# Attention and gated MoE on one core: TensorE's order in chunks 1 to 8 written by hand, a unit of attention every nine groups of products

## The chip, the cores and the metric

The kernel runs on one core of one Trainium2 chip. The metric is the device time of one execution in microseconds (us). Engines are named as in the profile: PE is TensorE (PEld its weight loads), DVE is VectorE, ACT is ScalarE, POOL is GpSimd, SP is the queue that issues the DMAs.

## The reference

q, k and v have the shape (8 batches, 8 heads, 576 tokens, 64). Attention is the sum of two parts, and its output x goes through a gated MoE layer.

```python
out_d = sm_attn(q_d, k_d, v_d)          # q, k, v averaged over 4 tokens: 144 each
out_up = np.repeat(out_d, 4, axis=2)
mask = np.abs(pos[:, None] - pos[None, :]) < 4
attn = softmax(where(mask, q @ k.T / 8, -1e9))
x = (out_up + attn @ v)                 # to (4608 tokens, 512)
gate = 1 / (1 + exp(-(x @ w_gate)))     # w_gate, w_val: 512 x 1536
return (gate * (x @ w_val)) @ w_out     # w_out: 1536 x 512
```

## The kernel before

**Attention** is done in 32 units, one for each pair of heads of a batch, four to a batch. A unit's work is cut into named steps: `prep2` (POOL sums q and k over four tokens), `s0` (PE: 48 small products, the local scores, then DVE adds the mask), `s1` and `sm` (softmax: DVE, POOL, ACT), `d0` (PE: 8 products, the scores `sd` of the averaged part, then DVE and ACT take their softmax), `dn`, `vd`, `v` (normalise; sum v; split v into two halves of 16 bits in `vblk`), `a0`, `a1` (PE transposes of the local softmax, into `at`), `at` (PE transposes of the averaged one, `adt`), `od` (PE: its product with v), and `x` (PE: the 30 products of the local softmax with `vblk`; DVE adds both parts into `xs`; ACT and POOL write two 16-bit halves of it to `xT`).

**MoE** is done in 9 chunks of 512 tokens. A chunk has 12 groups, and one group has three parts of 12 products with 512 columns: gate (`pg`), then value (`pv`), then output (`po`, for the group before). ACT takes the tanh of `pg` (L634), DVE multiplies it with `pv` (L642), ACT and DVE split the result (L650, L651), and `po` sums over the 12 groups. A chunk can begin once all units of its tokens have written `xT`: chunk 2 needs batch 2, chunk 3 batch 3, and so on to chunk 7, which needs batch 7.

**PSUM**: six banks belong to the MoE (`gate`, `val`, `o0` to `o3`). Attention's products of unit 4 and later, and the transposes that find a batch's largest v (`mxt`, in `max_all`), all take turns in two banks with the tag `att`. For the bound of a batch's v, `vmax` reads each unit's v on ACT, and after the fourth unit `max_all` makes a transpose, two DVE operations and a second product at once, and `pow2` and `inv_scaled` make the scales `pvb`, `svb`, `sxb` from it.

**Order.** Each step is put at a position, a number; the code emits the steps sorted by it. Chunk 0 lies below position `C1` = 56, with the conversion of the weights. From 56 on, each part of 12 products is one position: gate, value, output are 3, a chunk is 36, and chunk c begins at 56 + 36(c - 1). `base(u)` is a unit's position, and `offset(u, k)` that of its step k. The framework's scheduler decides at build time in which order every engine issues its instructions: the emitted order is a priority, and an instruction whose inputs or bank it holds to be late is overtaken by others. Loads go through SP, in three, one, one and five buffers for `qk`, `qkd`, `vd` and `v`.

`side_by_side` emits the small products of `s0` and `d0`, each tied behind the last, with one dummy product ahead of them (L404).

Of the kernel before, what the change touches and what calls it, by code (L numbers as in the profile page):

```python
# [10 lines left out]
F32 = mybir.dt.float32  # L11
I32 = mybir.dt.int32
AF = mybir.ActivationFunctionType
ALU = mybir.AluOpType
AX = mybir.AxisListType
# [1 line left out]

T = dict(ma=4.5, mas=0.45, mb=9.5, mbs=0.5, c1=56, gs=2.66, g0=16.84, r1=1.99, rs=1.6, ob=3.16, v0=15.13, v1=16.62, v2=17.5, vs=2.12, o0=18, os=1.2, pro=2.36, u4=13.82, u5=21, u6=27, u7=32, l4=1.3, l5=2.77, l6=9.47, l7=8.68, lv=15.08, vm=1.58, b8=6.75, s8=6.63, b12=26.05, s12=8.17, hold=32.07, al=0.76, am=1, z=3.68, sd=0, sn=0.79, v0m=0.61, xd=[2, 3, 7], ad=[0, 3, 7], aa=[0, 1, 2, 3, 6], td=[0, 3, 9, 10], vd=[0, 1, 2, 3, 6, 9, 10], a_prep2=-0.89, a_s0=0.01, a_s1=0.52, a_sm=1.82, a_d0=2.39, a_dn=5.17, a_a0=4.37, a_vd=4.6, a_a1=5.1, a_v=2.74, a_at=5.22, a_od=5.79, a_x=8.38, m_prep0=-3.14, m_prep2=-1.43, m_s0=0.69, m_s1=2.59, m_sm=3.12, m_d0=2.84, m_a0=10, m_dn=10.78, m_vd=11.67, m_a1=12, m_v=13.07, m_at=13.44, m_od=15.64, m_x=17, k0=30, k_prep2=0, k_s0=2, k_s1=2, k_sm=4, k_d0=3, k_dn=0, k_a0=3, k_vd=8, k_a1=2, k_v=5, k_at=0, k_od=0, k_x=0)  # L20
P = 128
B, H, S, D = 8, 8, 576, 64
NT = B * S
# [1 line left out]
NPAIR = H // 2  # L25
# [12 lines left out]
NCHUNK = NT // CH  # L38
NFC = DFF // P
# [11 lines left out]
VUP = 512.0  # L51
# [9 lines left out]
def attention_moe(ctx, tc, qk, qkd, v, vd, wg, wv, wo, mask, out):  # L61
    nc = tc.nc
# [55 lines left out]
    nc.vector.memset(ones, 1.0)  # L118


    def max_all(src, n):

        pt = ps_a.tile([P, 512], F32, tag="att", name=uniq("mxt"))
        nc.tensor.transpose(pt[:n, :P], src, ident)
        row = wk.tile([n, 1], F32, tag="mxr", name=uniq("mxr"))
        nc.vector.tensor_reduce(row, pt[:n, :P], axis=AX.X, op=ALU.max)
        dg = wk.tile([n, n], F32, tag="mxg", name=uniq("mxg"))  # L130
        nc.vector.tensor_scalar(out=dg, in0=ident[:n, :n], scalar1=row, scalar2=None, op0=ALU.mult)
        nc.tensor.matmul(pt[:, 256 : 256 + n], ones[:n, :].to_broadcast([n, P]), dg, start=True, stop=True)
        return pt[:, 256 : 256 + n]

    names = {}

    def uniq(k):
        names[k] = names.get(k, 0) + 1
        return f"{k}{names[k]}"

    def pow2(dst, src):

        got = max_all(src, src.shape[1])
        nc.vector.tensor_scalar(out=dst, in0=got, scalar1=TINY, scalar2=None, op0=ALU.max)
        nc.vector.tensor_scalar(
            out=dst.bitcast(I32), in0=dst.bitcast(I32), scalar1=EXPBITS, scalar2=None,
            op0=ALU.bitwise_and)

    def inv_scaled(dst, src, c):
        nc.vector.reciprocal(dst, src)  # L150
        nc.vector.tensor_scalar(out=dst, in0=dst, scalar1=c, scalar2=None, op0=ALU.mult)
# [145 lines left out]
    def vmax(u):  # L297
        b, hp = divmod(u, NPAIR)
        if hp == 0:
            vm[b] = wk.tile([P, NPAIR], F32, tag="vm", name=f"vm{b}")  # L300

        junk = wk.tile([P, NBLK * D], F16, tag="junk", name=f"junk_{u}", bufs=1)
        nc.scalar.activation(junk, vraw[u].rearrange("p a b -> p (a b)"), AF.Abs, accum_out=vm[b][:, hp : hp + 1])
        if hp == NPAIR - 1:
            m1 = wk.tile([P, 1], F32, tag="vm1", name=f"vm1_{b}")
            nc.vector.tensor_reduce(m1, vm[b], axis=AX.X, op=ALU.max)
            pow2(pvb[:, b : b + 1], m1)
            inv_scaled(svb[:, b : b + 1], pvb[:, b : b + 1], 2.0 * VUP)
            nc.vector.tensor_scalar(out=sxb[:, b : b + 1], in0=svb[:, b : b + 1], scalar1=4096.0 / VUP, scalar2=None, op0=ALU.mult)

    def batch_scales(b):
        nc.vector.tensor_scalar(
            out=tsc[:, b, :], in0=pw[:, 1::2], scalar1=pvb[:, b : b + 1], scalar2=2.0 ** -14,
            op0=ALU.mult, op1=ALU.mult)

    def out_scale(b):
        nc.vector.tensor_scalar(
            out=osc[:, b : b + 1], in0=qmax, scalar1=pw[:, 0:1], scalar2=pvb[:, b : b + 1], op0=ALU.mult, op1=ALU.mult)
# [82 lines left out]

    def side_by_side(other, mms):

        last = nc.tensor.matmul(other[:, 511:512], idle[:, :P], idle[:, :1], start=True, stop=True)  # L404
        for o, w, x in mms:
            with tc.issue_after(last.ins):
                last = nc.tensor.matmul(o, w, x, start=True, stop=True)  # L407

    owner = {}
    done = set()  # L410

# [213 lines left out]
    def moe_gate(c, fc):  # L625
        assert ("g", fc) in done
        assert all(u in done for u in range(min(NU, -(-(c + 1) * CH // S) * NPAIR))), (c, fc)
        x = xT[c]
        pt = ps_o.tile([P, CH], F32, tag="gate", name=f"pg_{c}_{fc}")
        for k in range(4):  # L630
            product(pt, [wg16[:, fc, a, k, :] for a in range(2)], [x[:, k, e, :] for e in range(2)], k == 0, k == 3)
        t = wk.tile([P, CH], F32, tag="tanh", name=f"tanh_{c}_{fc}")
        for b, o, n in segs_of_chunk(c):
            nc.scalar.activation(t[:, o : o + n], pt[:, o : o + n], AF.Tanh, scale=tsc[:, b, fc : fc + 1])  # L634
        return t
# [50 lines left out]
    def add(pos, f):  # L686
        steps.setdefault(pos, []).append(f)
# [6 lines left out]

    ALONE = {k[2:]: p for k, p in T.items() if k[:2] == "a_"}
    AMONG = {k[2:]: p for k, p in T.items() if k[:2] == "m_"}
    C1 = T["c1"]
    GSTEP = T["gs"]
    gt = {}
# [19 lines left out]
    def base(u):  # L719
        if u < NPAIR:  # L720
            return 1 + u * T["pro"]
        if u < 2 * NPAIR:
            return T[f"u{u}"]
        if u < 3 * NPAIR:
            return C1 - T["b8"] + (u - 2 * NPAIR) * T["s8"]
        return C1 + T["b12"] + (u - 3 * NPAIR) * T["s12"]

    def offset(u, k):
        if u < NPAIR:
            return ALONE[k] * T["al"]  # L730
        return AMONG[k] * (T["am"] if u < 2 * NPAIR else 1)

    for u in range(NU):
        b, hp = divmod(u, NPAIR)
        p0 = base(u)
        for k in ALONE if b == 0 else AMONG:
            add(p0 + offset(u, k), units[u][k])
            if b == 0 and T["k_" + k] and k in ("s0", "s1", "d0", "a0", "a1", "at", "od", "x"):
                add(p0 + offset(u, k), lambda n=T["k_" + k]: awake(n))
        if b == 0:  # L740
            if u == 0:
                add(-10, first_loads)
            add(2 + T["v0m"] * hp, lambda u=u: vmax(u))
            continue
        if b == 1:
            pl = p0 + offset(u, "prep0") - T[f"l{u}"]
            add(max(pl, base(u - 2) + offset(u - 2, "s1") + 0.1) if u > NPAIR + 1 else pl, lambda u=u: load_qk(u))
            add(T["lv"] + 0.2 * hp, lambda u=u: vload(u))
            after = base(u - 1) + 0.1 if u > NPAIR else 0
            add(max(pl + 0.5, after + offset(u - 1, "prep2") if after else 0), lambda u=u: load_qkd(u))  # L750
            add(max(pl + 0.5, after + offset(u - 1, "vd") if after else 0), lambda u=u: load_vd(u))
            add(T["lv"] + T["vm"] * (hp + 1), lambda u=u: vmax(u))
            continue
        add(base(u - 2) - 1 if b > 2 else max(base(u - 2) - 1, T["hold"]), lambda u=u: load_qk(u))
        add(base(u - 1) - 1 if u > 2 * NPAIR else T["hold"], lambda u=u: load_qkd(u))
        add(base(u - 1) + offset(u - 1, "vd"), lambda u=u: load_vd(u))
        pb = base(b * NPAIR)
        add(pb - 5 + hp, lambda u=u: vload(u))
        add(pb + hp, lambda u=u: vmax(u))

    worder.sort(key=lambda w: wpos(*w))
    add(RPOS, ratios)
# [3 lines left out]
    for n, (why, k, i) in enumerate(worder):  # L766
        add(wpos(why, k, i), lambda n=n: wstep(n))
    for b in range(1, B):
        add(max(base(b * NPAIR) + 5, C1 - 3), lambda b=b: (batch_scales(b), out_scale(b)))


    for fc in range(NFC):
# [6 lines left out]
    def run_steps(end):  # L779
        for p in sorted(p for p in steps if p < end):  # L780
            for f in steps.pop(p):
                f()
# [1 line left out]
    run_steps(C1)  # L784
    pos = C1
    prev = None
    for c in range(1, NCHUNK):
        for fc in range(NFC):
            t = moe_gate(c, fc)
            run_steps(pos + 1)  # L790
            moe_val(c, fc, t)
            run_steps(pos + 2)
            if prev is not None:
                moe_out(*prev)
            run_steps(pos + 3)
            pos += 3
            prev = (c, fc)
    moe_out(*prev)
    assert not steps


# [74 lines left out]
```

## Time and profile before

| | |
|---|---|
| median of 3 runs | 1142.66 us (1139.7 to 1144.16) |
| profiled execution, its own time | 1139.69 us |
| its span, first to last instruction | 1137.9 us |
| mean granted TensorE clock | 0.961 |
| busy: PE, DVE, ACT, POOL | 93%, 48%, 42%, 29% |

The profile is of one execution. A product's duration in it is longer than the distance to the next product, because products follow each other in a pipeline; the chain of waits gives the distance.

### The profile page before, as it was taken

To read this page: it belongs to the slowest core of one execution; us is meant where nothing else is said; L and a number is where in the kernel's file an instruction comes from. 1 tells how busy PE (TensorE), PEld (TensorE's weight loads), DVE (VectorE), ACT (ScalarE), POOL (GpSimd) and SP (SyncE) were. 2 spreads that over 40 slices of the span, in tenths; PEclk is the share of its full clock that TensorE was granted. 3 is DMA by queue.
4 is the path that set the end of the run, shared out by engine and by line. 5 is a ranking of instruction groups with operands and counts; after the bars stand their busy time and mean duration, and the time that the engine had idled before them with its cause. 6 is when DMAs were issued, how large, how long until landed. Compare 5 with 4: busy or idle time off the path is not lost.

```text
span 1137.9 us, 18103 instructions
## 1 busy us (share of the span) xinstructions
PE 1052.9 (93%) x7311; PEld 549.6 (48%) x7311; DVE 542.2 (48%) x954; ACT 482.1 (42%) x1176; POOL 335.5 (29%) x348
## 2 busy tenths in 40 slices
PE   6877788999996999899998999799989999999998
PEld 4753344545553555455444555455545554444443
DVE  5779999754436433543344433544354332122121
ACT  5734667533444443543444443534353443112112
POOL 6425546322235232332233233422343210000000
PEclk8659899999997999999999999999999999999999
DMA  9987675322114111321132211312120000000000
GB/s 348 391 298 242 236 247 180 138 103 68 57 60 153 52 53 55 114 75 61 64 105 70 69 54 64 127 48 69 57 90 19 1 1 38 1 1 38 1 1 37
DMA packets 32083, 110.48 MB, mean 97 GB/s; under 512 B 3584, under 2 KB 3840, under 8 KB 32000
## 3 DMA queue, kind: packets, MB, share of 16 engines
q1 hardware_dynamic: 32000, 109.33, 27.5%
q8 instruction: 57, 0.93, 0.3%
q14 instruction: 26, 0.21, 0.1%
HBM read 99.88 MB, written 9.44 MB: 96 GB/s over the span
## 4 chain that ended last, share of the span: by engine, by line
PE 80%; DVE 9%; ACT 4%; DMA 2%; POOL 2%; issue 2%; SPq 0%; DVEq 0%; ACTq 0%; POOLq 0%
PE po L400 23%; PE pg L400 23%; PE pv L400 22%; PE x L400 3%; PE od L400 2%; PE at L554 2%; PE s L407 2%; PE sd L407 1%; DVE wrv L209 1%; DVE wrv L210 1%; PE adt L565 1%; DMA v<-in_v_dram 1%; DVE vdblk L391 1%; DVE hmx L154 1%; ACT vblk L158 1%
## 5 line engine op out<-in xcount | busy, mean ns | idle before, releaser
L400 PE MATMUL pg<-xT,wg 128*128 128x512 f16 x1296 | 317.0, 387 | 21.7 <-ACT tanh L634 7.6
L400 PE MATMUL pv<-xT,wv 128*128 128x512 f16 x1296 | 310.9, 382 | 6.3 <-ACT wv L216 3.4
L400 PE MATMUL po<-g,wo 128*128 128x512 f16 x1188 | 278.7, 379 | 0.0
L400 PEld LDWEIGHTS <-wg 128*128 128x128 f16 x1296 | 124.7, 99 | 170.5 <-issue 23.5
L400 PEld LDWEIGHTS <-wv 128*128 128x128 f16 x1296 | 124.1, 98 | 154.4 <-issue 9.5
L400 PEld LDWEIGHTS <-wo 128*128 128x128 f16 x1296 | 123.9, 98 | 153.6 <-ACT wo L158 7.3
L642 DVE SCALAR_TENSOR_TENSOR tanh<-tanh,pv 128x512 f32<-128x512 f32 x108 | 73.7, 683 | 204.2 <-PE pv L400 192.7
L634 ACT ACTIVATE tanh<-pg,tsc 128x512 f32<-128x512 f32 (+7 forms) x192 | 86.6, 496 | 177.4 <-PE pg L400 177.2
L650 ACT ACTIVATE g<-tanh,gs 128x512 f16<-128x512 f32 x99 | 71.4, 721 | 151.9 <-DVE tanh L642 151.5
L651 DVE SCALAR_TENSOR_TENSOR g<-tanh,gs,g 128x512 f16<-128x512 f32 x99 | 81.8, 826 | 63.5 <-ACT g L650 63.0
L485 POOL TENSOR_TENSOR t<-t,mx 128x768 f32<-128x768 f32 x32 | 47.9, 1496 | 106.8 <-DVE mx L484 106.7
L597 DVE TENSOR_TENSOR xs<-x,od 128x464 f32<-128x464 f32 (+1 forms) x56 | 24.8, 455 | 95.1 <-PE x L400 94.8
L608 POOL TENSOR_TENSOR xT<-xs,xT 128x384 f16<-128x384 f32 (+7 forms) x54 | 45.5, 848 | 83.0 <-ACT xT L606 82.8
L496 POOL TENSOR_TENSOR t<-t,sm 128x768 f32<-128x768 f32 x28 | 46.3, 1654 | 72.8 <-DVE sm L494 65.3
L389 POOL TENSOR_TENSOR qkd<-qkd 128x576 f32<-128x576 f32 x29 | 36.2, 1248 | 80.9 <-DMA qkd<-in_qkd_dram 80.9
L158 ACT ACTIVATE vblk<-v,svb 64x640 f16<-64x640 f32 x48 | 39.6, 826 | 29.9 <-PE x L400 24.5
L391 POOL TENSOR_TENSOR vdblk<-vd 64x192 f32<-64x192 f32 x50 | 30.0, 600 | 72.1 <-PE od L400 66.7
L159 DVE SCALAR_TENSOR_TENSOR vblk<-v,svb,vblk 64x640 f16<-64x640 f32 x48 | 46.0, 959 | 11.0 <-ACT vblk L158 10.0
L474 DVE SCALAR_TENSOR_TENSOR t<-s,mk 128x384 f32<-128x384 f32 x64 | 32.8, 551 | 33.8 <-PE s L407 33.6
L539 POOL TENSOR_TENSOR ad<-e,sme 72x288 f32<-72x288 f32 x52 | 35.0, 693 | 45.8 <-PE adt L565 42.2
L522 ACT ACTIVATE e<-sd,mxd 72x144 f32<-72x144 f32 x128 | 47.0, 371 | 1.3
L491 DVE TENSOR_REDUCE sm<-t 128x12 f32<-128x768 f32 x32 | 30.4, 950 | 32.5 <-ACT t L486 32.5
(296 smaller groups left out, 1109.8 us busy)
## 6 DMA issues: line engine op xcount, KB each, us to landing
qk<-in_qk_dram SPq DMA_DIRECT2D x30, 610.0 KB, 4.2
qkd<-in_qkd_dram SPq DMA_DIRECT2D x29, 576.0 KB, 3.8
vd<-in_vd_dram SPq DMA_DIRECT2D x29, 384.0 KB, 3.0
v<-in_v_dram SPq DMA_DIRECT2D x32, 320.0 KB, 2.9
out_dram<-osb SPq DMA_DIRECT2D x16, 512.0 KB, 2.8
wo<-in_qk_dram SPq DMA_DIRECT2D x2, 610.0 KB, 9.8
wo<-in_qkd_dram SPq DMA_DIRECT2D x2, 576.0 KB, 9.2
out_dram<-osb SPq DMA_DIRECT2D x4, 256.0 KB, 2.3
```

What stands on the lines that cost most here:

```text
L158: nc.scalar.activation(hi, src, AF.Copy, scale=sc)
L159: nc.vector.scalar_tensor_tensor(out=lo, in0=src, scalar=sc, in1=hi, op0=ALU.mult, op1=ALU.subtract)
L391: eng.tensor_tensor(out=o, in0=x[ps, :, 0], in1=x[ps, :, 1], op=ALU.add)
L400: nc.tensor.matmul(o, w[a], x[c], start=first and i == 0, stop=last and i == len(pairs) - 1)
L485: nc.gpsimd.tensor_tensor(out=t, in0=t, in1=mx.unsqueeze(2).to_broadcast([P, 4 * NH, WIN]), op=ALU.subtract)
L496: eng.tensor_tensor(out=t, in0=t, in1=sm.unsqueeze(2).to_broadcast([P, 4 * NH, WIN]), op=ALU.mult)
L522: nc.scalar.activation(s["e"][:, qb, h, :], pt[:QM, qb * SD : (qb + 1) * SD], AF.Exp, bias=mx[:, qb : qb + 1], scale=QKSCALE / 16, accum_o ...
L608: eng.tensor_tensor(out=x[:, hp, 1, o : o + n], in0=src, in1=x[:, hp, 0, o : o + n], op=ALU.subtract)
L634: nc.scalar.activation(t[:, o : o + n], pt[:, o : o + n], AF.Tanh, scale=tsc[:, b, fc : fc + 1])
L642: nc.vector.scalar_tensor_tensor(out=t, in0=t, scalar=1.0, in1=pt, op0=ALU.add, op1=ALU.mult)
L650: nc.scalar.activation(g[:, 0], t, AF.Copy, scale=gs[:, fc : fc + 1])
L651: nc.vector.scalar_tensor_tensor(out=g[:, 1], in0=t, scalar=gs[:, fc : fc + 1], in1=g[:, 0], op0=ALU.mult, op1=ALU.subtract)
```

## The change

1. From chunk 1 on, the loop over chunks and groups stands in a region in which PE's instructions are issued in the order in which the code emits them. Other engines, and the place of PE instructions that are emitted before the region (chunk 0, units 4 to 7, the first steps of units 8 and 9), stay with the scheduler.
2. Units 8 to 31 begin every nine positions: `base(u)` = 44 + 9(u - 8). Before, units 8 to 11 were 6.63 apart from 49.25 on, and units 12 to 31 were 8.17 apart from 82.05 on.
3. Their steps take offsets of a new table, `STEADY`.
4. For batches 2 to 7 the bound of v is made in two steps: `vrows` (the transpose and two DVE operations) at 5.5 after the batch's first unit, and `vscale` (the second product, in a bank of its own, and the scales) at 6.65. Batch 1 keeps both at once; the scales of batches 2 to 7 for the MoE follow at 7 instead of 5.
5. In the region `side_by_side` has neither the dummy product nor the ties.

```diff
-... b8=6.75, s8=6.63, b12=26.05, s12=8.17, ...
+... b8=12, s8=9, ...
-    def max_all(src, n):
+    def max_rows(src, n):
         pt = ps_a.tile([P, 512], F32, tag="att", name=uniq("mxt"))
         nc.tensor.transpose(pt[:n, :P], src, ident)
...
+        return dg, pt
+    def spread(dg, n, pt=None):
+        if pt is None:
+            pt = ps_a.tile([P, 512], F32, tag="att", name=uniq("mxt"))
         nc.tensor.matmul(pt[:, 256 : 256 + n], ones[:n, :].to_broadcast([n, P]), dg, start=True, stop=True)
         return pt[:, 256 : 256 + n]
+        if hp == NPAIR - 1 and b < 2:
+            vrows(b)
+            vscale(b)
+    def vrows(b):
+        m1 = wk.tile([P, 1], F32, tag="vm1", name=f"vm1_{b}")
+        nc.vector.tensor_reduce(m1, vm[b], axis=AX.X, op=ALU.max)
+        vm[b] = max_rows(m1, 1)
+    def vscale(b):
+        pow2(pvb[:, b : b + 1], spread(vm[b][0], 1, vm[b][1] if b < 2 else None))
+        inv_scaled(svb[:, b : b + 1], pvb[:, b : b + 1], 2.0 * VUP)
...
-        last = nc.tensor.matmul(other[:, 511:512], idle[:, :P], idle[:, :1], start=True, stop=True)
+        last = None if ordered else nc.tensor.matmul(other[:, 511:512], idle[:, :P], idle[:, :1], start=True, stop=True)
         for o, w, x in mms:
+            if last is None:
+                nc.tensor.matmul(o, w, x, start=True, stop=True)
+                continue
...
+    STEADY = dict(prep0=0, prep2=-3.5, s0=0, s1=0.1, sm=1.1, d0=2, dn=6.1, vd=9.4, v=8.2,
+                  a0=13, a1=13, at=14.4, od=15.6, x=16.6)
-        if u < 3 * NPAIR:
-            return C1 - T["b8"] + (u - 2 * NPAIR) * T["s8"]
-        return C1 + T["b12"] + (u - 3 * NPAIR) * T["s12"]
+        return C1 - T["b8"] + (u - 2 * NPAIR) * T["s8"]
...
+        if hp == NPAIR - 1:
+            add(pb + 5.5, lambda b=b: vrows(b))
+            add(pb + 6.65, lambda b=b: vscale(b))
-        add(max(base(b * NPAIR) + 5, C1 - 3), lambda b=b: (batch_scales(b), out_scale(b)))
+        add(max(base(b * NPAIR) + (5 if b < 2 else 7), C1 - 3), lambda b=b: (batch_scales(b), out_scale(b)))
...
+    ordered.append(True)
+    with tc.manual_schedule(engines={mybir.EngineType.PE}):
         for c in range(1, NCHUNK):
```

## Rows read from the trace of the kernel before

**Rows 1.** The page: busy time (share of the span) and instructions of each engine

```profile
PE 1052.9 (93%) x7311; PEld 549.6 (48%) x7311; DVE 542.2 (48%) x954; ACT 482.1 (42%) x1176; POOL 335.5 (29%) x348
```

**Rows 2.** Windows by chunk: length; PE, PEld, DVE, ACT, POOL; clock; DMA, GB/s

```profile
231.90:346.80 114.90, 112.89 (x835) 57.87 (x834) 50.92 (x94) 49.03 (x128) 29.48 (x32) 1.00 0.24 80
346.80:482.90 136.10, 123.40 (x1012) 65.15 (x1012) 62.35 (x115) 59.98 (x157) 48.57 (x55) 0.95 0.23 77
482.90:601.10 118.20, 113.71 (x859) 59.61 (x859) 50.82 (x93) 52.40 (x135) 38.88 (x44) 0.99 0.23 77
601.10:721.80 120.70, 113.93 (x860) 58.81 (x860) 50.93 (x93) 52.26 (x135) 39.14 (x44) 0.99 0.22 73
721.80:841.40 119.60, 112.67 (x861) 58.54 (x861) 52.03 (x93) 51.72 (x133) 39.59 (x45) 1.00 0.22 73
841.40:951.90 110.50, 109.28 (x754) 56.34 (x753) 45.80 (x73) 44.88 (x114) 26.34 (x31) 1.00 0.05 17
951.90:1137.90 186.00, 181.46 (x840) 82.10 (x839) 37.04 (x52) 38.78 (x68) 0.63 (x1) 1.00 0.04 15
```

**Rows 3.** Chain of waits at the start of chunk 4: start, us, what

```profile
601.63 2.91 DMA v<-in_v_dram
...
605.39 0.74 ACT tanh L634 x2
...
606.17 4.44 PE pg L400 x12
```

**Rows 4.** Waits of PE from 231.9 on: total us, times, longest

```profile
PE pg L400 <- ACT tanh L634: 7.6, 6, 2.7
...
PE s L404 <- DVE xs L597: 6.3, 5, 3.8
PE mxt L132 <- DVE mxg L131: 3.0, 5, 0.6
```

**Rows 5.** Chain of waits through undisturbed units of chunk 2

```profile
420.41 0.65 PE x L400 x24
...
424.73 0.16 PE x L400 x6
...
429.45 0.86 PE s L407 x48
...
431.93 2.59 PE pg L400 x12
...
435.17 0.33 PE at L554 x3
...
440.70 0.65 PE sd L407 x8
...
447.60 0.38 PE adt L565 x6
...
452.73 0.73 PE od L400 x6
453.47 0.66 PE x L400 x24
```

**Rows 6.** Timeline: last reader of the score banks; a late reader of `at`

```profile
431.35 1.01 DVE L474 SCALAR_TENSOR_TENSOR t<-s,mk 128x384 f32<-128x384 f32 x2
...
443.42 0.36 ACT L522 ACTIVATE e<-sd,mxd 72x144 f32<-72x144 f32 x1
...
603.26 0.49 PE L554 MATMUL at<-ident,t 128*128 128x128 f32 x3
...
606.75 0.45 DVE L548 TENSOR_TENSOR at<-at,at 128x290 f16<-128x290 f32 x1
```

**Rows 7.** Chain of waits around the first gate of chunk 1

```profile
229.05 0.39 PE x L400 x4
...
233.77 0.86 PE s L407 x48
```

**Rows 8.** Timeline of SP near the last weight loads

```profile
194.25 0.42 SPq L286 DMA_DIRECT2D v<-in_v_dram  x1
```

More of the change, by code (lines that the diff above doesn't have):

```diff
@@ L16 @@
 PSUM = bass.MemoryType.PSUM
-T = dict(ma=4.5, mas=0.45, mb=9.5, mbs=0.5, c1=56, gs=2.66, g0=16.84, r1=1.99, rs=1.6, ob=3.16, v0=15.13, v1=16.62, v2=17.5, vs=2.12, o0=18, os=1.2, pro=2.36, u4=13.82, u5=21, u6=27, u7=32, l4=1.3, l5=2.77, l6=9.47, l7=8.68, lv=15.08, vm=1.58, b8=6.75, s8=6.63, b12=26.05, s12=8.17, hold=32.07, al=0.76, am=1, z=3.68, sd=0, sn=0.79, v0m=0.61, xd=[2, 3, 7], ad=[0, 3, 7], aa=[0, 1, 2, 3, 6], td=[0, 3, 9, 10], vd=[0, 1, 2, 3, 6, 9, 10], a_prep2=-0.89, a_s0=0.01, a_s1=0.52, a_sm=1.82, a_d0=2.39, a_dn=5.17, a_a0=4.37, a_vd=4.6, a_a1=5.1, a_v=2.74, a_at=5.22, a_od=5.79, a_x=8.38, m_prep0=-3.14, m_prep2=-1.43, m_s0=0.69, m_s1=2.59, m_sm=3.12, m_d0=2.84, m_a0=10, m_dn=10.78, m_vd=11.67, m_a1=12, m_v=13.07, m_at=13.44, m_od=15.64, m_x=17, k0=30, k_prep2=0, k_s0=2, k_s1=2, k_sm=4, k_d0=3, k_dn=0, k_a0=3, k_vd=8, k_a1=2, k_v=5, k_at=0, k_od=0, k_x=0)
+T = dict(ma=4.5, mas=0.45, mb=9.5, mbs=0.5, c1=56, gs=2.66, g0=16.84, r1=1.99, rs=1.6, ob=3.16, v0=15.13, v1=16.62, v2=17.5, vs=2.12, o0=18, os=1.2, pro=2.36, u4=13.82, u5=21, u6=27, u7=32, l4=1.3, l5=2.77, l6=9.47, l7=8.68, lv=15.08, vm=1.58, b8=12, s8=9, hold=32.07, al=0.76, am=1, z=3.68, sd=0, sn=0.79, v0m=0.61, xd=[2, 3, 7], ad=[0, 3, 7], aa=[0, 1, 2, 3, 6], td=[0, 3, 9, 10], vd=[0, 1, 2, 3, 6, 9, 10], a_prep2=-0.89, a_s0=0.01, a_s1=0.52, a_sm=1.82, a_d0=2.39, a_dn=5.17, a_a0=4.37, a_vd=4.6, a_a1=5.1, a_v=2.74, a_at=5.22, a_od=5.79, a_x=8.38, m_prep0=-3.14, m_prep2=-1.43, m_s0=0.69, m_s1=2.59, m_sm=3.12, m_d0=2.84, m_a0=10, m_dn=10.78, m_vd=11.67, m_a1=12, m_v=13.07, m_at=13.44, m_od=15.64, m_x=17, k0=30, k_prep2=0, k_s0=2, k_s1=2, k_sm=4, k_d0=3, k_dn=0, k_a0=3, k_vd=8, k_a1=2, k_v=5, k_at=0, k_od=0, k_x=0)
 P = 128
@@ L131, in max_all @@
         nc.vector.tensor_scalar(out=dg, in0=ident[:n, :n], scalar1=row, scalar2=None, op0=ALU.mult)
+        return dg, pt
+    def spread(dg, n, pt=None):
+        if pt is None:
+            pt = ps_a.tile([P, 512], F32, tag="att", name=uniq("mxt"))
         nc.tensor.matmul(pt[:, 256 : 256 + n], ones[:n, :].to_broadcast([n, P]), dg, start=True, stop=True)
         return pt[:, 256 : 256 + n]
+    def max_all(src, n):
+        dg, pt = max_rows(src, n)
+        return spread(dg, n, pt)
     names = {}
@@ L139, in uniq, with pow2 @@
         return f"{k}{names[k]}"
-    def pow2(dst, src):
-        got = max_all(src, src.shape[1])
+    def pow2(dst, got):
         nc.vector.tensor_scalar(out=dst, in0=got, scalar1=TINY, scalar2=None, op0=ALU.max)
@@ L303, in vmax @@
         nc.scalar.activation(junk, vraw[u].rearrange("p a b -> p (a b)"), AF.Abs, accum_out=vm[b][:, hp : hp + 1])
[L304 to L309, printed above, removed]
+        if hp == NPAIR - 1 and b < 2:
[8 more added lines that the diff above has]
+        inv_scaled(svb[:, b : b + 1], pvb[:, b : b + 1], 2.0 * VUP)
+        nc.vector.tensor_scalar(out=sxb[:, b : b + 1], in0=svb[:, b : b + 1], scalar1=4096.0 / VUP, scalar2=None, op0=ALU.mult)
     def batch_scales(b):
@@ L402, in side_by_side @@
     def side_by_side(other, mms):
-        last = nc.tensor.matmul(other[:, 511:512], idle[:, :P], idle[:, :1], start=True, stop=True)
+        last = None if ordered else nc.tensor.matmul(other[:, 511:512], idle[:, :P], idle[:, :1], start=True, stop=True)
         for o, w, x in mms:
+            if last is None:
+                nc.tensor.matmul(o, w, x, start=True, stop=True)
+                continue
             with tc.issue_after(last.ins):
                 last = nc.tensor.matmul(o, w, x, start=True, stop=True)
+    ordered = []
     owner = {}
@@ L696, in attention_moe @@
     AMONG = {k[2:]: p for k, p in T.items() if k[:2] == "m_"}
+    STEADY = dict(prep0=0, prep2=-3.5, s0=0, s1=0.1, sm=1.1, d0=2, dn=6.1, vd=9.4, v=8.2, a0=13, a1=13, at=14.4, od=15.6, x=16.6)
     C1 = T["c1"]
@@ L730, in offset @@
             return ALONE[k] * T["al"]
-        return AMONG[k] * (T["am"] if u < 2 * NPAIR else 1)
+        if u < 2 * NPAIR:
+            return AMONG[k] * T["am"]
+        return STEADY[k]
     for u in range(NU):
@@ L786, in attention_moe @@
     prev = None
[L787 to L798, printed above, removed]
+    ordered.append(True)
+    with tc.manual_schedule(engines={mybir.EngineType.PE}):
+        for c in range(1, NCHUNK):
+            for fc in range(NFC):
+                t = moe_gate(c, fc)
+                run_steps(pos + 1)
+                moe_val(c, fc, t)
+                run_steps(pos + 2)
+                if prev is not None:
+                    moe_out(*prev)
+                run_steps(pos + 3)
+                pos += 3
+                prev = (c, fc)
+        moe_out(*prev)
     assert not steps
```

## The prediction

> **What bounds the kernel now.** I read the page first: PE is busy 93% of the span and no other engine half of it [rows 1]. Then the windows from one chunk's first gate to the next [rows 2]. The six stretches of chunks 1 to 6 hold the same products, 36 x 12 = 432 each, and about four units each, yet they take 114.9, 136.1, 118.2, 120.7, 119.6 and 110.5 us. In the last one the chunks 7 and 8 run nearly without attention. So something other than products and attention fills up to 25 us of a chunk, and the second row also has a mean clock of 0.95. DVE, ACT and POOL are under 50% in all seven rows.
>
> The chain of waits says what. Inside a chunk it runs from PE instruction to PE instruction, 2.59 us for 12 products, with attention's pieces between them [rows 5]. At a chunk's start it leaves PE [rows 3]: the batch's last unit has only just been done, and the gate of chunk 4 waits for a tanh, which stood on ACT behind a read of v, whose load landed then. The 12 products after it take 4.44 us instead of 2.59: the window of that chunk has a mean clock of 0.99 [rows 2], so for part of them the clock stood on its lower level, 1.2 instead of 2.4 GHz, after PE had stood idle. The waits of PE name the same places [rows 4]: `pg` for tanh, `s` for `xs`, the two halves of `max_all` for each other.
>
> **What full work would take.** Chunks 1 to 8 have 96 groups of 36 products, 3456 in all. The last window holds 840 of them, so 2616 lie before it. At 2.59 / 12 = 0.2158 us that is 564.6 us. A unit costs, by its pieces, s 0.86, sd 0.65, two transposes of 0.33, adt 0.38, od 0.73, x 0.65 + 0.16: 4.09 us [rows 5]; 24 units, 98.2. Five bounds of v, two short pieces each, at the 0.33 of three transposes a piece: 3.3. Together 666.1 us, where the first six windows of rows 2 took 720.0. **53.9 us are lost** between 231.9 and 951.9. The last window is full already: 840 products in the 181.46 us that PE is busy there are 0.216 a product.
>
> The idle part of the loss is smaller than that: in the six windows PE is idle 720.0 - 685.9 = 34.1 us [rows 2]. The rest is time in which PE counts as busy and does half: the 12 products of 4.44 us lose 1.85 [rows 3]. The Trainium skill, in "Trainium Kernel Development and Optimization", section Performance Expectations, calls matmul busy time a bad metric because matmuls are pipelined. By the busy rows alone there would be 34 us to win and my sum below would end near 1118; the count of products gives 53.9, and the even last window bears the count out.
>
> **The change part by part.**
>
> *Spacing.* Units of 9 positions make four units exactly one chunk of 36. The fourth unit of batch 2 has x at 44 + 27 + 16.6 = 87.6, and chunk 2 begins at 92, and so with each later chunk. 4.4 positions are at least 4.4 x 2.59 = 11.4 us, for a tail of xs, cast and difference that took 2.5 us at chunk 1's start (x ends 229.44, the gate comes at 231.9) [rows 2, 7]. If the order holds, no gate waits for its unit. Loads: v's at -5 to -2 from a batch's start take buffers freed by a `v` step at -9.8 or earlier (five buffers, 9 apart). The wait of rows 3, in which ACT stands behind a load of v, goes too.
>
> *Fixed order.* Now every PE wait in the region is a wait of all that follows, so each place must have room. In steady state the two banks are used, in turn, by s at 0, sd at 2, the transposes of the unit before at 4, adt at 5.4, od at 6.6, x at 7.6, s again at 9. Between s and sd, and between sd and the transposes, lie two parts, 5.2 us; from transposes to adt, adt to od and od to x one part, 2.6 us. What the readers need: DVE finished with s 432.36 - 430.31 = 2.05 us after it; the last exp of sd ended 443.78, 2.43 after sd [rows 5, 6]. These fit twice over. The tightest is the bank of the transposes: the slowest reader that I found ended 607.20, 3.5 us after them (603.75) [rows 6], 0.9 over the room, but it stood behind the same late load of v. Inputs that come through long chains (softmax for `a0`, 13 positions, over 33 us after `s0`) have far more. So I put what is left at 0.2 us per unit, 24 x 0.2 = 5 us; bounds 0 and 1 us a unit, 0 to 24 us.
>
> *Dummy product and bound of v.* A unit loses two dummies of one column; at 0.86 / 48 = 0.018 us, the price of a small product of s [rows 5], all 48 are 0.9 us, which I leave out; no reason speaks for a loss. The two halves of `max_all` cost 0.6 us of waiting each time [rows 4]; with a gate part of 2.59 between `vrows` (5.5) and `vscale` (6.65) that is covered, and it is in the 53.9. An extra bank turn per batch falls between adt and od and needs one short DVE read. `svb` is needed by `v` at 8.2, 1.5 positions or 4 us after `vscale`, against a handful of small DVE operations (0.6 us for two with their waits, so some 2). If this cover were gone, ACT and DVE would be late with `vblk`, whose reader x comes 8.4 positions later: nothing for PE.
>
> *Earlier start of units 8 and 9.* This is the part with a cost. u8's `s0`, `d0` move from 49.9 and 52.1 to 44 and 46, u9's to 53 and 55: all below 56, and in the banks' turn ahead of unit 7's adt (45.44), od (47.64) and x (49). Now u8's s runs after u7's x, at 233.77, and those 2.5 us from u7's x to chunk 1's gate leave no slack [rows 2, 7]. In the new turn s takes 0.86, DVE frees its banks 2.05 after, sd takes 0.65, its exps 2.43: 6.0 us that u7's x can be later. PE has output parts of chunk 0 to fill it, but only those that it has now, so the delay shows at the gate. On the other side are waits hidden under fill, and 1.5 us of PE work done before. Then `a0` of unit 8, fixed two parts after chunk 1's first gate, waits in the region for the banks behind u9's s and sd, another 0 to 5 us. DVE has some 4 us more to do there (estimated as four passes like the 1.01 of rows 6); the steps between s and sd that hold the banks are in the 6.0 already, so I count at most 1. The loads of v for units 8 to 11 go out five positions earlier, ahead of more of the last weight loads on SP: an issue takes 0.42 us of SP [rows 8], so four delay those by 1.7 at most. Bounds together: a gain of 3 (s and sd of both units, 1.51 us each, in gaps that PE has now) to a loss of 6.0 + 5 + 1 + 1.7 = 13.7; between them I take a loss of 5, nearer the middle, since half of the bank delay can be covered.
>
> **Sum.** 231.9 + 666.1 + 186.0 = 1084.0; + 5 at the start of chunk 1; + 5 within the units: span 1094. The profiled execution takes 1.8 us over its span: 1096. The median of the three runs was 3.0 above the profiled execution; I forecast 1098 for the median.
>
> **Rivals.**
>
> *A. The hand-over costs more, or units leave more.* Loss of 13.7 at chunk 1 and 0.6 us per unit, 14.4: 1084.0 + 28 + 1.8 = 1114, to 1125 with the bounds. For it: the region cannot be overtaken, and unit 7 has no slack [rows 7]. Against it: the measured releases [rows 6].
>
> *B. Slower: the two banks can't turn in nine positions.* In the undisturbed stretch x of one unit lies 33.1 us before x of the next (the chain has it at 420.41 and 453.47), while nine positions and a unit make 9 x 2.59 + 4.09 = 27.4. If 33.1 is what the banks need, and not what the scheduler chose, a fixed order pays 5.7 us a unit, 137 us: 1084 + 5 + 137 = 1226 span, about 1229. It decides from a mean of (1137.9 - 1089) / 24 = 2.0 us a unit on. For it: the pieces there stand about two parts apart, as if each waited for a bank. Against it: the bank is free 2.0 to 2.5 us after the products [rows 5, 6], so the hardware wasn't what held them. The Trainium skill, "TensorE: Matmul & The Clock Gate", section Part 2, says that matmuls stay in program order and only weight loads are pulled ahead. The trace agrees: gates wait up to 2.7 us for tanh, and no other product fills that time [rows 4]. It holds in both kernels, and by it each wait in the fixed order costs in full.
>
> *C. No change.* The waits at chunk starts have moved into the units: the same 53.9, 2 us a unit, 1138 span, 1140 to 1143 median. For it: the tail of a batch's bound and of softmax could itself be late. Against it: DVE, ACT and POOL under 50% [rows 2].
>
> **Chances.** Forecast (1084 to 1106) 0.60; A (1106 to 1126) 0.22; C 0.08, half of it still 0.5% faster; B 0.07; better than 1084 0.03. I call 0.5% (5.7 us) what a measurement can tell. Faster 0.88, same 0.05, slower 0.07. The range that leaves out 2 in 10 reaches from 1084, where both charges are nothing, to 1122, into A; the likeliest case's own is 1084 to 1106.
>
> **What would show it.** Right: the windows by chunk become even, about 111 us for chunks 1 to 6 (93.2 of products, 16.4 of units, 0.7, and 0.8 of residue), with the last two unchanged; the lower clock gone after chunk 1's start; `pg` no longer waiting for tanh or xT; PE's idle time after 231.9 under 15 us. The start of chunk 1 lies near 235, and u8's s ahead of u7's adt. Wrong: `at`, `adt` or `sd` waiting over 1 us in every unit for a reader on DVE or ACT (B); the first gate of chunk 1 after 246 (A); chunks still at 118 us with small waits (C).

## The result, and the profile after

The changed kernel takes 1106.81 us (median of 4 runs, 1104.77 to 1107.43), the kernel before 1141.65 in the same comparison: ratio 0.9691, interval 0.9666 to 0.9715, so faster by 3.1%. The profiled execution took 1106.37 us, its span is 1104.6. The forecast was 1098, in a range of 1084 to 1122. The time lies inside the range, but just past the upper end of the likeliest case (1106), in the times that were given to rival A (1106 to 1126, chance 0.22).

The same line of the page as in [rows 1]: PE is busy 5.5 us less, the span is 33.3 shorter.

```profile
PE 1047.4 (95%) x7267; PEld 546.4 (49%) x7267; DVE 539.8 (49%) x954; ACT 476.6 (43%) x1176; POOL 348.4 (32%) x348
```

The windows from one chunk's first gate to the next, to be set beside [rows 2] (length; PE, PEld, DVE, ACT, POOL; clock; DMA, GB/s). Left out are chunks 3 to 5, which are like chunk 2. Output products of one chunk run in the window of the next, not at the same places as before, so only the rows of equal content (chunks 2 to 5) are read one by one.

```profile
230.00:360.60 130.60, 121.45 (x936) 64.48 (x934) 64.78 (x121) 55.92 (x149) 44.87 (x48) 0.93 0.25 83
360.60:471.60 111.00, 111.00 (x854) 57.86 (x853) 52.05 (x93) 51.78 (x134) 40.82 (x44) 1.00 0.24 80
...
804.40:911.50 107.10, 107.10 (x739) 55.39 (x738) 39.56 (x69) 42.60 (x110) 24.20 (x27) 1.00 0.06 20
911.50:1104.60 193.10, 189.19 (x877) 85.55 (x875) 38.19 (x54) 41.57 (x75) 0.00 (x0) 1.00 0.04 17
```

From chunk 2 to chunk 6 PE is busy for every microsecond, at a clock of 1.00, and chunks 2 to 5 last 110.9 to 111.0 us each, where before they took 118 to 136. Chunk 1 takes 130.6: there are 9.2 us of idle time and a mean clock of 0.93. The only other idle time is 3.9 us of the last window, which had 4.5 before. So what is still lost to waits is in chunk 1, at the hand-over from the part that the scheduler orders to the region of fixed order.

The waits of PE from 226 on (total us, times, longest), to be set beside [rows 4]; two more are of 0.4 and 0.2 us. None lies behind 263, so the three groups of rows 4 are gone and what is left belongs to the start of chunk 1:

```profile
PE at L571 <- ACT e L539: 4.1, 2, 2.4
PE sd L417 <- DVE t L491: 2.1, 1, 2.1
PE od L413 <- ACT e L539: 1.6, 1, 1.6
PE s L423 <- DVE pvb L150: 0.5, 1, 0.5
```

The chain of waits there (start, us, what), to be set beside [rows 7]:

```profile
223.57 0.86 PE s L423 x48
...
229.29 0.38 PE adt L582 x6
...
230.12 1.94 PE pg L413 x9
232.07 0.69 PE sd L423 x8
...
233.75 0.56 ACT e L539 x3
...
234.35 1.00 PE od L413 x6
235.35 2.83 PE x L413 x16
...
241.36 3.49 PE pv L413 x12
...
247.41 0.88 DVE vblk L165
248.29 0.93 DVE t L491 x2
...
254.44 0.73 ACT e L539 x4
...
255.22 0.90 PE at L571 x3
256.12 0.93 PE adt L582 x6
257.05 4.16 PE pg L413 x12
```

Unit 8's `s` (223.57) now runs ahead of unit 7's adt, and its `sd` ahead of unit 7's od and x. So od waits 1.64 us for the exp that reads `sd`, and x ends at 239.0, 9.6 later than before [rows 7]. The first gate doesn't wait for that: it starts at 230.0, since nine products of it go ahead of `sd`. Its last three wait for unit 7's `xT` and start at 239.67. The timeline of PE (start, us, line, output from inputs; in brackets the idle time before it and who ended it) has both:

```profile
235.30 3.72 PE L413 MATMUL x<-at,vblk 128*128 128x58 f32 x20
...
239.67 1.69 PE L413 MATMUL pg<-xT,wg 128*128 128x512 f16 x3 [0.22 <-ACT xT L623]
```

The rest of the delay shows behind it. Unit 9's `s` can only run at 245.76, behind a wait for the bound of batch 2 (`pvb`). Its readers on DVE stand behind a `vblk` (248.29), `sd` waits 2.12 for them, and the transposes of unit 8, which have a fixed place behind both, wait 2.45 and 1.68 us for the exps. The last of these exps stood on ACT behind a read of v, whose load landed at 252.86.

The same stretch in windows of 6 us (columns as above):

```profile
232.00:238.00 6.00, 4.37 (x32) 3.94 (x31) 1.99 (x5) 2.44 (x12) 2.55 (x5) 0.85 0.55 201
238.00:244.00 6.00, 5.63 (x18) 2.43 (x18) 2.69 (x6) 1.60 (x4) 3.50 (x4) 0.58 0.11 39
244.00:250.00 6.00, 2.98 (x64) 1.95 (x62) 4.78 (x13) 2.37 (x3) 0.00 (x0) 0.99 0.28 104
250.00:256.00 6.00, 1.87 (x8) 1.00 (x6) 3.29 (x8) 3.92 (x16) 2.14 (x2) 0.50 0.43 142
256.00:262.00 6.00, 6.00 (x27) 3.29 (x27) 1.49 (x5) 1.68 (x5) 2.39 (x3) 0.66 0.03 11
```

Between 244 and 256 PE works 4.85 of 12 us, although the next gate's products, whose inputs the group before has already read, could run: their place is behind the transposes. The granted clock falls twice: to 0.58 in the second row, behind a row in which PE was busy for 4.37 of 6 us, and to 0.50 (1.2 GHz) in the fourth, behind one with 2.98. In the fifth, where PE is busy throughout, it is still 0.66, a mix of the two levels: 12 products take 4.16 us (257.05) instead of 2.59. The Trainium skill, "TensorE: Matmul & The Clock Gate", section Part 2, says that matmuls stay in program order; the trace agrees, no product passes the waiting transposes.

### The profile page after: what moved, and what is told of

The parts are those of the page before. It is cut to its first block, busy times and chain, and to the rows that moved or that the text cites. A ratio compares the mean times of both kernels' runs of the same rounds, so it can differ in the third digit from the quotient of the medians.

```text
span 1104.6 us, 18045 instructions
## 1 busy us (share of the span) xinstructions
PE 1047.4 (95%) x7267; PEld 546.4 (49%) x7267; DVE 539.8 (49%) x954; ACT 476.6 (43%) x1176; POOL 348.4 (32%) x348
## 4 chain that ended last, share of the span: by engine, by line
PE 85%; DVE 7%; ACT 2%; DMA 2%; POOL 2%; issue 1%; SPq 0%; DVEq 0%; ACTq 0%
PE po L413 25%; PE pg L413 24%; PE pv L413 24%; PE x L413 4%; PE od L413 2%; PE at L571 2%; PE s L420 2%; PE sd L420 1%; PE adt L582 1%; DVE vdblk L404 1%; DVE wrv L216 1%; DVE hmx L160 1%; POOL wg L223 1%; POOL t L513 1%; ACT e L539 1%
## 5 line engine op out<-in xcount | busy, mean ns | idle before, releaser
L413 PE MATMUL pg<-xT,wg 128*128 128x512 f16 x1296 | 308.4, 387 | 9.2 <-ACT wg L222 4.6
L413 PE MATMUL pv<-xT,wv 128*128 128x512 f16 x1296 | 302.2, 382 | 5.3 <-ACT wv L222 3.7
L413 PE MATMUL po<-g,wo 128*128 128x512 f16 x1188 | 272.4, 379 | 0.0
L668 DVE SCALAR_TENSOR_TENSOR g<-tanh,gs,g 128x512 f16<-128x512 f32 x99 | 78.1, 789 | 40.8 <-ACT g L667 37.8
L625 POOL TENSOR_TENSOR xT<-xs,xT 128x384 f16<-128x384 f32 (+7 forms) x54 | 53.7, 1011 | 55.6 <-ACT xT L623 55.6
L402 POOL TENSOR_TENSOR vd<-vd 128x384 f32<-128x384 f32 x29 | 30.0, 1035 | 77.5 <-DMA vd<-in_vd_dram 77.5
L165 DVE SCALAR_TENSOR_TENSOR vblk<-v,svb,vblk 64x640 f16<-64x640 f32 x48 | 53.2, 1109 | 0.9 <-ACT vblk L164 0.2
L571 PE MATMUL at<-ident,t 128*128 128x128 f32 x192 | 30.7, 296 | 13.7 <-DVE t L513 5.0
```

What stands on the lines that cost most here:

```text
L165: nc.vector.scalar_tensor_tensor(out=lo, in0=src, scalar=sc, in1=hi, op0=ALU.mult, op1=ALU.subtract)
L402: nc.gpsimd.tensor_tensor(out=x[:, :, 0:2], in0=x[:, :, 0:2], in1=x[:, :, 2:4], op=ALU.add)
L413: nc.tensor.matmul(o, w[a], x[c], start=first and i == 0, stop=last and i == len(pairs) - 1)
L571: nc.tensor.transpose(o, s["t"][:, par, i], ident)
L625: eng.tensor_tensor(out=x[:, hp, 1, o : o + n], in0=src, in1=x[:, hp, 0, o : o + n], op=ALU.subtract)
L668: nc.vector.scalar_tensor_tensor(out=g[:, 1], in0=t, scalar=gs[:, fc : fc + 1], in1=g[:, 0], op0=ALU.mult, op1=ALU.subtract)
```

## The experiments

Each run was timed against the kernel before on the same chip. Beside order alone, spacing alone, start at 47 and four groups free the kernel before took 1146.48 us, beside the others 1139.56 to 1141.65, so the ratios of these four come out lower; versions of the changed kernel are compared by their medians. Medians and ratios:

| run | median us | ratio to before, interval |
|---|---|---|
| changed kernel | 1106.81 | 0.9691 [0.9666, 0.9715] |
| changed kernel, again | 1105.02 | 0.9692 [0.9675, 0.9709] |
| order alone | 1160.75 | 1.0129 [1.0073, 1.0186] |
| spacing alone | 1127.05 | 0.9835 [0.9776, 0.9894] |
| old offsets | 1110.22 | 0.9724 [0.9686, 0.9761] |
| bound of v at once | 1109.35 | 0.9730 [0.9713, 0.9747] |
| dummies kept | 1105.74 | 0.9695 [0.9677, 0.9713] |
| four groups free | 1101.66 | 0.9619 [0.9558, 0.9680] |
| start at 47 | 1093.76 | 0.9545 [0.9495, 0.9595] |
| start at 47, again | 1093.94 | 0.9579 [0.9550, 0.9608] |
| hand-over moved | 1096.01 | 0.9617 [0.9596, 0.9638] |
| read of v tied | 1105.22 | 0.9682 [0.9651, 0.9713] |
| start at 47, read tied | 1093.72 | 0.9580 [0.9550, 0.9608] |

**Order alone.** The kernel before, with nothing but the region:

```diff
-    for c in range(1, NCHUNK):
+    with tc.manual_schedule(engines={mybir.EngineType.PE}):
+        for c in range(1, NCHUNK):
```

> The kernel before with one part of the change: the loop over chunks 1 to 8 stands in the region of fixed PE order, positions and offsets stay as before. Theory (order and places are both needed: a fixed order pays only where each step's bank is free in time): attention no longer bunches at a chunk's start, but its old places leave od and sd, and x and the transposes, without a part between them, so each unit waits some 0.5 to 1.5 us; 1084 of full work + 12 to 36 in units + some 8 at the start of chunk 1, about 1105 to 1130. Rival (the order alone is the gain): at or below the changed kernel, 1090 to 1107. Rival (the spacing alone is the gain): as before, 1137 to 1147, or slower.

Measured 1160.75: slower than before by 1.3%, and 31 us above the theory's range. Only the rival that gives the gain to the spacing alone allowed for a slower kernel, and the next run shows that the spacing alone isn't the gain either. The largest waits of PE from 226 on:

```profile
PE s L404 <- DVE xs L597: 12.1, 18, 1.0
PE at L554 <- ACT e L522: 9.9, 10, 3.5
PE mxt L127 <- ACT e L522: 8.6, 4, 2.8
```

And one place of it in the timeline of PE:

```profile
413.32 0.98 PE L400 MATMUL x<-at,vblk 128*128 128x58 f16 x30
414.94 0.16 PE L404 MATMUL s<-idle 128*128 128x1 bf16 x1 [0.64 <-DVE xs L597]
415.12 0.93 PE L407 MATMUL s<-qk 64*64 64x64 f32 x48
...
422.11 0.71 PE L407 MATMUL sd<-qks 64*72 64x144 f32 x8 [0.44 <-DVE at L548]
...
426.19 0.55 PE L554 MATMUL at<-ident,t 128*128 128x128 f32 x3 [0.67 <-ACT e L522]
```

At 8.17 positions a unit, x of one unit and `s` of a later one fall on one place, with no product between, and `s` waits for `xs` to empty the bank, 18 times. The transposes, `sd` and the second transposes follow with one part between them, and the last two wait too. By the chain of waits, `sd` stands there behind a read of v on ACT, whose load took 3.06 us from 416.99, so not every wait of this run comes from the spacing. In the kernel before, where the scheduler may put products between them, the wait of `s` for `xs` comes 5 times [rows 4]. PE stands idle 925.70 - 870.65 = 55 us behind chunk 1's first gate, against 906.00 - 867.34 = 39 in the kernel before.

**Spacing alone.** The changed kernel with `if True:` in place of the region, and with dummies and ties. The new offsets and the split bound stay, so this is all of the change but the order:

> The changed kernel without the region, so the scheduler orders PE from the new positions, with the dummy products back. Theory: the scheduler still holds attention back to the chunk's start, because it plans from its own times and not from the places; the waits of 10 to 20 us at four or five chunk starts stay, 1130 to 1145. Rival (spacing alone is the gain): 1100 to 1112, with even windows by chunk.

Measured 1127.05, 19.4 us (1.65%) under the kernel before that was timed beside it, 14.6 under that of the first comparison, of the 35 of the whole change. That lies between the theory (1130 to 1145) and its rival (1100 to 1112). Windows of chunks 1 and 2:

```profile
229.70:341.40 111.70, 108.87 (x778) 56.83 (x777) 50.13 (x93) 47.02 (x123) 32.82 (x36) 1.00 0.22 71
341.40:464.70 123.30, 119.31 (x918) 62.81 (x917) 53.20 (x101) 54.52 (x140) 41.28 (x46) 0.94 0.25 80
```

Waits of PE from 226 on:

```profile
PE pg L413 <- ACT tanh L651: 3.6, 2, 2.4
PE pg L413 <- POOL xT L625: 2.7, 5, 1.0
```

The waits at the chunks' starts are not gone: those for tanh are 3.6 us instead of 7.6 [rows 4], those for `xT` come 5 times. The scheduler still chooses the order and lets a unit's pieces lag: chunk 1's window has 778 PE instructions and chunk 2's 918, where the fixed order has 853 or 854 in each even chunk. Neither part alone is the change: -1.65% and +1.3% by themselves, -3.1% together.

**Old offsets.** Units nine apart, fixed order, but the old table for their steps:

```diff
-        return STEADY[k]
+        return AMONG[k]
```

> The changed kernel with the old table of offsets for the steps of units 8 to 31, and all else changed. u's local transposes then stand one part behind the next unit's s, and one part ahead of its sd, instead of two parts after sd. Theory (the new places count only where a part less leaves no room): DVE's 2.05 us for s fit into one part of 2.59, exps of 2.4 to 3.4 us don't always, so 0.3 to 1 us a unit, 7 to 24 us more than the changed kernel, 1112 to 1130. Rival (the spacing of nine alone makes the room): within 4 us of it.

Measured 1110.22, 3.4 to 5.2 above the changed kernel's two medians, with intervals that overlap. The theory (1112 or more) is missed, and the rival (within 4 us) is about right: most of the room comes from the spacing. Chunk 2 takes 112.8, the next 112.3; `at` waits for the exps six times:

```profile
PE at L571 <- ACT e L539: 3.5, 6, 1.0
```

Of the 50 us between this run and order alone most must come from the spacing, since the split bound, another difference, is worth 4 (below) and the dummies nothing; that is argued, since no run changes the spacing by itself.

**Bound of v at once.**

```diff
-        if hp == NPAIR - 1 and b < 2:
+        if hp == NPAIR - 1:
             vrows(b)
             vscale(b)
...
-        pow2(pvb[:, b : b + 1], spread(vm[b][0], 1, vm[b][1] if b < 2 else None))
+        pow2(pvb[:, b : b + 1], spread(vm[b][0], 1, vm[b][1]))
...
-        if hp == NPAIR - 1:
-            add(pb + 5.5, lambda b=b: vrows(b))
-            add(pb + 6.65, lambda b=b: vscale(b))
```

> The changed kernel with the bound of v made at once again, three positions after the batch's first unit (transpose, two DVE operations, second product, with no part between). Theory: each of five batches pays the bare wait between the two products, 0.6 us, and up to 2 us where sd's exps still hold the bank or the fourth read of v is not done: 3 to 10 us more than the changed kernel. Rival (the split was needed for nothing else than form, the bank and ACT being free there): within 2 us of it.

Measured 4.3 us above the changed kernel that was timed beside it (1105.02). One wait is new, up to 0.6 us for each of six batches, and has most of that size; chunk 2 takes 111.7 instead of 111.0, and in chunk 1, where other waits change too, 132.5 instead of 130.6:

```profile
PE mxt L135 <- DVE mxg L128: 3.8, 6, 0.6
```

**Dummies kept.** The dummy product is made in the region as well, without ties:

```diff
-        last = None if ordered else nc.tensor.matmul(...)
+        last = nc.tensor.matmul(...)
+        last = None if ordered else last
```

> The changed kernel with the dummy product kept ahead of s and sd in the region. Theory: the banks are free at these places, so 44 dummies cost their own time, 0.02 us each: 0 to 2 us more. Rival (the dummy waits for the second bank, as in the run of the order alone, where PE waited 12.1 us there): 8 us more or over.

Measured 1105.74 against 1105.02: no difference.

**Start at 47.** Unit 8 three positions later, and all behind it:

```diff
-b8=12
+b8=9
```

> The changed kernel with units 8 to 31 three positions later (b8 = 9 instead of 12). u9's s and sd then stand in the region, and u8's sd behind unit 7's x. Theory (the changed kernel's remaining 20 us over full work are the hand-over: u8's and u9's early products ahead of unit 7 in the two banks, then unit 8's transposes fixed behind u9's): two thirds of it go, about 1092 to 1098; the fourth unit's x is 1.4 positions, 3.6 us, ahead of its chunk, against a tail of 2.5 us, so the later chunk starts cost 0 to 1 us each. Rival (the remainder is the weights' conversion or the chip's clock there): 1103 to 1110, unchanged.

Measured 1093.76, and 1093.94 in the repeat. Windows of chunks 1 and 2:

```profile
228.60:345.80 117.20, 114.58 (x879) 61.55 (x878) 61.09 (x116) 54.31 (x146) 40.83 (x45) 0.99 0.26 85
345.80:456.70 110.90, 110.90 (x852) 57.84 (x851) 52.57 (x93) 51.12 (x135) 41.20 (x44) 1.00 0.25 81
```

Timeline of PE at the hand-over:

```profile
228.98 0.90 PE L413 MATMUL od<-adt,vdblk 128*128 128x144 f32 x6
229.72 1.89 PE L413 MATMUL x<-at,vblk 128*128 128x58 f32 x16
...
234.25 0.71 PE L423 MATMUL sd<-qks 64*72 64x144 f32 x8
...
237.92 1.87 PE L420 MATMUL s<-qk 64*64 64x64 f32 x48
239.72 3.38 PE L413 MATMUL pv<-xT,wv 128*128 128x512 f16 x12
```

Unit 7's od and x run ahead of unit 8's `sd` again and wait for nothing; unit 9's `s` comes at its place in the region. Chunk 1 falls from 130.6 to 117.2, by 13.4, and the time by 11 to 13; the other chunks stay at 111. So the loss of chunk 1 was the hand-over, and not the conversion of the weights or the chip's clock there, as the rival had it; three positions decide over most of it.

**Four groups free.** The region begins four groups later, so that the scheduler orders the hand-over:

```diff
+    FREE = 4
...
+    todo = [(c, fc) for c in range(1, NCHUNK) for fc in range(NFC)]
+    for c, fc in todo[:FREE]:
+        group(c, fc)
     ordered.append(True)
     with tc.manual_schedule(engines={mybir.EngineType.PE}):
+        for c, fc in todo[FREE:]:
+            group(c, fc)
...
```

> The changed kernel with the first four groups of chunk 1 outside the region, so the scheduler may reorder PE across the hand-over. Theory: the waits of the fixed order there go (unit 8's transposes for the banks, about 8 to 10 us with the lower clock that follows), unit 7's od behind u8's exps stays (some 4 to 6): 1094 to 1101. Rival (bank turn and not the fixed order makes the loss): under 4 us less than the changed kernel, 1102 to 1108.

Measured 1101.66, 3.4 to 5.2 under the changed kernel's two medians and at the edge between the theory (to 1101) and its rival (from 1102). At the hand-over the waits of `sd` and of the transposes are gone and od's 1.64 us stay, as the theory had it. But a bunch of the same kind stands at the new border:

```profile
273.89 0.16 PE L417 MATMUL sd<-idle 128*128 128x1 bf16 x1 [0.92 <-DVE t L491]
...
277.92 0.90 PE L571 MATMUL at<-ident,t 128*128 128x128 f32 x3 [2.76 <-ACT e L539]
```

At both borders that were tried, the pieces that are emitted ahead of the region lag, and the first fixed piece of attention waits for them.

**Hand-over moved.** Start at 47, with the steps around the border set by hand:

```diff
+    HANDOVER = {(8, "v"): 57.5, (9, "s0"): 58.1, (9, "s1"): 58.2, (9, "sm"): 59.2, (9, "d0"): 59.1}
...
-            add(pb + 5.5, lambda b=b: vrows(b))
-            add(pb + 6.65, lambda b=b: vscale(b))
+            add(pb + 5.5 if b > 2 else 56.2, lambda b=b: vrows(b))
+            add(pb + 6.65 if b > 2 else 57.05, lambda b=b: vscale(b))
...
-        add(max(base(b * NPAIR) + (5 if b < 2 else 7), C1 - 3), lambda b=b: (batch_scales(b), out_scale(b)))
+        add(max(base(b * NPAIR) + (5 if b < 2 else 11 if b == 2 else 7), C1 - 3), lambda b=b: (batch_scales(b), out_scale(b)))
```

> Units three positions later as in the run that starts at 47, and at the hand-over the bound of batch 2 moved into the region behind chunk 1's first gate and value, u8's split of v behind it, u9's s and sd at 58.1 and 59.1 with a part ahead of each. Theory (the 7 us that were left there are fixed places whose banks hang on u8's sd and on the bound, with no product between): 4 to 6 us go, 1087 to 1091 (about 0.950 of the kernel before). Rival (the rest is not the order but work that must be done there): 1092 to 1096, as the run that starts at 47.

Measured 1096.01: no gain over start at 47, and that theory falls. One wait went from the bound to the transposes, and the lower clock follows it (12 products in 4.44 us instead of 2.75 in the timeline, a granted clock of 0.72 from 256 to 262). The profile is of the slowest of five executions, 1100.14:

```profile
254.94 0.55 PE L571 MATMUL at<-ident,t 128*128 128x128 f32 x3 [2.19 <-ACT e L539]
255.32 4.44 PE L413 MATMUL po<-g,wo 128*128 128x512 f16 x12
```

**Read of v tied.** The chain showed the late exp behind ACT's read of v. Here that read, for batches 3 to 7, stands behind the `g` at its own position:

```diff
...
+        if b > 2:
+            with tc.issue_after(last_g[0].ins):
+                read()
+        else:
+            read()
...
+        last_g[0] = nc.scalar.activation(g[:, 0], t, AF.Copy, scale=gs[:, fc : fc + 1])
```

> The changed kernel, in which ACT's read of v for the bound of batches 3 to 7 is tied behind the group's g of its position, so that ACT doesn't take it as soon as its load is out. Theory (at the hand-over ACT stands behind such a load, 250.17 to 252.86, and u9's exps, which hold the banks, stand behind ACT): 2.7 us of wait go, and with the clock that falls after it 3 to 6 us, 1099 to 1102; nothing moves after 262, where PE has no such wait. Rival (the bank turn behind u9's s and sd is late enough by itself): within 1.5 us of the changed kernel.

Measured 1105.22, no gain. The wait of `at` fell from 4.1 to 3.1 us, and the time not at all:

```profile
PE at L578 <- ACT e L546: 3.1, 2, 2.3
```

So the read was last in the chain, and what it held was worth 1 us of a wait: the banks behind unit 9's late `s` and `sd` are late without it, and `sd` still waits 2.1 us for `t`, as the rival had it. The same edit on start at 47, and two plain repeats:

> Units three positions later (start at 47), and the read of v tied as in the run beside it. Theory: there the load holds ACT from 241.74 to 244.71 and a wait of only 0.4 us is left for the transposes, so less is to be won: 0 to 3 us under the untied one, 1090 to 1094.

> The run that starts at 47 once more, beside the tied one: 1092 to 1096, of the kernel before 0.955 to 0.962.

> The changed kernel once more, beside the three that follow, so that differences of under one per cent can be read: 1104 to 1109, of the kernel before 0.966 to 0.972.

They gave 1093.72, 1093.94 and 1105.02. The best version is the changed kernel with `b8=9`: 11 us below it by the medians of the repeats, ratio to before 0.9579 against 0.9692.

## Why the prediction was nearly right, and where it was off

**Full work and the even chunks: right.** About 111 us were forecast for chunks 1 to 6, and chunks 2 to 5 take 110.9 to 111.0. The loss of 53.9 us was real and could be won outside the hand-over. Chunk 6 and the last window are not unchanged: 300.2 us together instead of 296.5, with 33 more products of 512 columns in them. Two counts were off by little: behind 231.9 there are six bounds of v and not five, at 0.11 + 0.31 us each by the chain, 2.5 and not 3.3; and the first six windows of rows 2 hold 432 to 445 products, not 432 each, which the sum, made from the total of 2616, doesn't use.

**Within the units: the right size, for another reason.** The pieces and products of a chunk were counted at 93.2 + 16.4 + 0.7 = 110.3; 111.0 is 0.7 more for four units, 0.17 a unit against 0.2 forecast, 4.2 us if all 24 are like these. The 0.2 stood for waits that are left, and there is none behind 263. The chain shows what it is: the twelve products behind `s` take 2.70 us instead of 2.59, and those behind `sd` 2.69 (443.49), 0.1 each, twice a unit. That the size came out is luck.

```profile
267.93 2.59 PE pg L413 x12
270.52 0.86 PE s L420 x48
271.38 2.70 PE pv L413 x12
```

**The hand-over at chunk 1: mis-sized.** Forecast 5, bounds -3 to 13.7. The span is 1104.6 - 1084.0 = 20.6 over full work; less the 4.2 above, 16.4 are left for it. Chunk 1's own window bears this out: it is 19.6 longer than a steady chunk. It holds work that a steady chunk doesn't have, at full clock 0.73 + 2.12 for unit 7's od and x (its 20 products of 32 bits took 1.73 + 0.39 us in the kernel before), 0.65 for `sd` of unit 8, 1.51 for `s` and `sd` of unit 9 and 0.42 for a second bound, 5.4 in all; and it has eleven output products less, 2.4 us, since the region's first group has none before it. That makes 3.0 of work, so 16.6 are lost. This is the term that failed, and its upper bound too: 16.4 - 5 = 11.4 too much there, 0.8 too little within the units, together the 10.6 by which the span of 1094 was missed. The median was missed by 8.8 only, because it lies 2.2 above the span, where 4 had been added.

Two things were not in the term. First, the bank turn costs more and doesn't end with unit 7: its x ended 9.6 late, not 6.0, and I gave 0 to 5 us to `a0` and 1 at most to DVE, yet `sd` waits 2.5 for `t` and the transposes 4.1 for the exps, because readers of the late `s` and `sd` stand behind `vblk` on DVE. Second, I counted idle time alone. Of the 16.6, idle are 9.2, which is within the bounds; the other 7.4, which carry the term past them, went while PE counts as busy. Six rows show most of it, against the same pieces at full clock: `pg` 4.16 and 2.59, `pv` 3.49 and 2.59, two transposes of 0.90 and 0.55, adt 0.93 and 0.38, sixteen products of x 2.83 and 1.73, the last three of the first gate 1.69 and 0.81 make 1.57 + 0.90 + 0.70 + 0.55 + 1.10 + 0.88 = 5.7. I had read that very effect in rows 3 and left it out of my own bound. In start at 47 the window of chunk 1 is 6.2 over a steady one: 2.6 idle, 1.5 for work by the same count (od and x of unit 7, `sd` of unit 8 and a bound, less the output products), and some 1.6 for `s` (1.87 instead of 0.93) and `pv` (3.38 instead of 2.75, both by the timelines) at the lower clock (granted 0.75 from 238 to 244), 5.7 in all. Whether that rest can be had by another order stays open; the two edits that aimed at it got none of it.

So half of rival A came, the hand-over, past the 13.7 that A gave it; the other half, 0.6 us a unit, did not. The time still fell into the range because its upper end, 1122, left room for units that cost more, and they took 4.2 us: that is luck.

**Where it would show: half right.** I had chunk 1's first gate near 235, and set 246 as the sign of rival A. It came at 230.0, earlier than before, and the cost of A came all the same, 15 us later. The order inside the region is fixed among its own instructions, while those emitted before it find places between them: nine products of the gate, which don't read unit 7's `xT`, could go ahead of its x. The sign to watch was the window of chunk 1, not its start. PE's idle time behind the first gate is 874.60 - 861.53 = 13.1, under the 15 forecast.

**Spacing and order.** That nine positions leave room for the banks is shown by the chunks 2 to 6 without a wait; that a fixed order pays for its waits, by order alone. Rival B was wrong for nine positions; at 8.17 its mechanism, banks that aren't free in time, has a large part in what makes order alone slower than before (12.1 us of waits of `s` for `xs`, against 6.3 in the kernel before). The chunk starts need both parts: with spacing alone the gates still wait for tanh and xT.

**Bound of v, dummies: right.** The split is worth 4.3 us, where I counted 0.6 of waiting a batch, 3.6 for six, as part of the loss; the dummies nothing.

**The read of v.** Rows 3 named it at chunk 4, and the chain named it again at 252.86. Tying it gained nothing there, so the last link of a chain isn't yet its cause.

## What to carry to other kernels

A fixed order for one engine pays only when the places in it leave room for the readers of every shared buffer; test it at the spacing that you mean to use, since the same order with the old spacing and offsets was 1.3% slower and with the new ones 3% faster than before. Size the border between a scheduled and a fixed stretch by itself: list what is emitted ahead of the border and still unfinished there, in the turn of the banks, and move the first unit until the old ones are through (three positions were worth 11 us). Price a wait of TensorE as its idle time and what the lower clock takes behind it, for which the count of work per window is the measure, not the busy time.

## Not expected

The size of what comes behind a wait: beside 9.2 us of idle time in chunk 1 at least 5.7 were lost in busy time. The clock is granted at 0.50 from 250 to 256, where PE waits, and still at 0.66 from 256 to 262, where PE is busy for all of the 6 us. In the steady chunks, without waits, it is 1.00.
